# Attention scores of two pieces of keys, or of two groups of queries, in one visit of the matrix engine

## The chip, the core and the metric

The kernel runs on one core of a Trainium2 chip. The metric is device time in microseconds of the whole kernel, the median of the runs. Engines are called as in the profile: PE is the matrix engine (PEld its weight loads), DVE the vector engine, ACT the scalar engine, POOL the general-purpose engine, SP the engine whose queue issues the DMAs here. PSUM is the memory that PE writes to, in banks; SBUF is the working memory.

## What is computed

Four batches of 12480 tokens with 128 features, and 49 agents per batch, all in float32. Agents attend to the keys, queries attend to the agents, and the result runs through two matrices with a squared relu between them.

```
scale = 1 / sqrt(128)
def sm(a, b):
    s = scale * (a @ b.transpose(0, 2, 1))
    s = s - s.max(-1, keepdims=True)
    e = exp(s)
    return e / (e.sum(-1, keepdims=True) + 1e-9)
agent_v = sm(agents, k) @ v           # (4, 49, 128)
attn = sm(q, agents) @ agent_v        # (4, 12480, 128)
r = maximum(attn @ w_in, 0)           # w_in 128 x 2048
out = (r * r) @ w_out                 # w_out 2048 x 128
```

## The kernel before

**The tokens.** A batch is cut into `NS` = 13 pieces of 960 tokens (`G` = 8 columns of `CH` = 120 tokens). The same cut serves keys and values (pieces) and queries (groups; 52 of them over the four batches, `NSG`).

**The main loop** has one block per group of queries and per sixteenth of the hidden layer and half of the tokens: 52 x 16 = 832 blocks, called i. The product of `agent_v` and `w_in` is folded into one small matrix per batch (`w_make`), so that a block is: `mm1(i)` (L376, matmuls on L384), six matmuls from the softmax of the queries `PT` into a bank pair `h`; `relu(i)` on ACT (L390); after every second block `square` on ACT (L393), `high` on DVE (L397, a rounded copy) and `low` on DVE (L401, what the rounding left), each over the two blocks; and `mm2` (L403, matmuls on L412), twelve matmuls, five blocks behind `mm1` (`LAG`). After eight blocks one tile of the output is whole, and `store` (L414) takes it out with a copy on ACT (L417) and an addition on DVE (L418). `h` has two buffers, so `mm1(i)` needs `relu(i - 2)` to be through. `rg`, `gh` and `gl` have three.

**PSUM.** The output tiles use two bank pairs in turn, `pairs`; while one collects an output, the other is free for all other matmuls ("visits"), and `bank()` hands it out. So a visit's result has to be read before the next visit writes there.

**The work beside the main loop**, for which the visits are:
- *A piece of keys:* `k_load` (L158), `k_scores` (L168, through `scores`, L162, matmuls on L165: 8 columns in two halves of 64 and 56 tokens, 49 agents wide, into one bank), `k_copy` on ACT (L172) into the tile `sk`, `k_pmax` on DVE (L175), the maximum over the piece for every agent and partition. When the 13 pieces of a batch are there, `k_max` (L180) takes the maximum over them.
- *A piece of values:* `k_sub` on POOL (L197), `k_exp` and `k_hi` on ACT, `k_lo` on POOL (L207), `v_hi` on ACT, `v_lo` on DVE, `v_acc` on PE (L239), `v_sum` on DVE (L255).
- *A group of queries:* `q_load` (L298), `q_scores` (L302), then `q_shift` (L320), which is the maximum over the agents (`q_max`, L314) and its subtraction (`q_sub`, L318) on DVE; `q_exp` on ACT (L325); `q_inverse` on DVE (sum L329, two small steps L333 and L334); `q_norm` on POOL (L337, the multiplication); `q_hi` on ACT (L341, a rounded copy) and `q_lo` on POOL (L344, the rest); `q_transpose` on PE (L352) and `q_copy` on ACT (L356); `q_spread`, two DMAs.

**The order** is written out by a planner, and every engine runs its instructions in the order of emission. Each step gets a time in blocks (`at`), and the steps are emitted sorted by time. `chain` (L439) places a list of steps one behind the other, with `hop` (L431) as the least distance in blocks between two engines; each step of an engine takes one block's place on it (`taken`), and PE's visits stand only behind three blocks of every eight (`slots`). A step on PE and the readers of its bank (`reads_bank`, L474) are placed together: the last reader may stand at most one block later. A DVE step that reads a bank directly behind PE stands at +0.47 of PE's block, and the pair's `low` is then moved behind it (`read`, L625); other steps stand at +0.5, `high` at +0.6 and `low` usually at +0.65 of an odd block. `plan_tokens` (L476) places a group of queries, `plan_batch` (L486) a batch's keys and values. Before the loop stands a hand-timed prologue with the first batch's attention and groups 0 and 1 (L531 on).

Of the kernel before, what the change touches and what calls it, by code (L numbers as in the profile page):

```python
# [25 lines left out]
def agent_attention_relu2_kernel(ctx: ExitStack, tc: tile.TileContext, qT, kT, v, agT, w_in, w_out, outT):  # L26
# [29 lines left out]
    ag_sb = cpool.tile([P, B, A], F32, name="ag_sb")  # L56
# [81 lines left out]
    H = G // 2  # L138
# [16 lines left out]
    def piece(n):  # L155
        return sk[:, n * G:(n + 1) * G, :]
# [5 lines left out]
    def scores(ps, x, b, cs=range(G)):  # L162
        for c in cs:
            for r in rc:
                nc.tensor.matmul(ps[r, 0, c * A:(c + 1) * A], x[:, c, r], ag_sb[:, b, :], start=True, stop=True)  # L165
# [5 lines left out]
    def k_copy(n):
        nc.scalar.copy(piece(n), pss.pop(("k", n)))  # L172

    def k_pmax(n):
        nc.vector.tensor_reduce(out=pm[:, n, :], in_=piece(n).rearrange("p c a -> p a c"), axis=AX.X, op=ALU.max)  # L175

    def k_pmax_bank(n):
        nc.vector.tensor_reduce(out=pm[:, n, :], in_=pss["k", n].rearrange("p c a -> p a c"), axis=AX.X, op=ALU.max)  # L178

    def k_max(step):  # L180
        if step == 0:
            nc.vector.tensor_reduce(out=m1, in_=pm[:, :NS - 1].rearrange("p n a -> p a n"), axis=AX.X, op=ALU.max)
        elif step == 1:
            nc.vector.tensor_tensor(m1, m1, pm[:, NS - 1], op=ALU.max)
# [111 lines left out]
    PT, qs, es, mxs, sms, pps = {}, {}, {}, {}, {}, {}  # L296
# [5 lines left out]
    def q_scores(s):  # L302
        pss["q", s] = scores(bank(), qs.pop(s), s // NS)

    def q_scores_part(s, x):
        if x == 0:
            pss["q", s] = bank()
            scores(pss["q", s], qs[s], s // NS, range(H))
        else:
            pss["q", s] = scores(pss["q", s], qs.pop(s), s // NS, range(H, G))  # L310

    def q_max(s):
        mxs[s] = wk.tile([CH, G, 1], F32, name="mx")
        nc.vector.tensor_reduce(out=mxs[s], in_=pss["q", s], axis=AX.X, op=ALU.max)  # L314

    def q_sub(s):
        es[s] = wk.tile([CH, G, A], F32, name="e")
        nc.vector.tensor_tensor(es[s], pss.pop(("q", s)), mxs.pop(s).to_broadcast([CH, G, A]), op=ALU.subtract)  # L318
# [5 lines left out]
    def q_exp(s):
        nc.scalar.activation(es[s], es[s], AF.Exp, scale=scale)  # L325

    def q_sum(s):
        sms[s] = wk.tile([CH, G, 1], F32, name="sm")
        nc.vector.tensor_reduce(out=sms[s], in_=es[s], axis=AX.X, op=ALU.add)  # L329

    def q_inverse(s):
        q_sum(s)
        nc.vector.tensor_scalar_add(sms[s], sms[s], 1e-9)  # L333
        nc.vector.reciprocal(sms[s], sms[s])  # L334

    def q_norm(s, eng=nc.gpsimd):
        eng.tensor_tensor(out=es[s], in0=es[s], in1=sms.pop(s).to_broadcast([CH, G, A]), op=ALU.mult)  # L337

    def q_hi(s):
        pps[s] = ppb[s % 2]  # L340
        nc.scalar.copy(pps[s][:, :, :A], es[s])  # L341

    def q_lo(s, eng=nc.gpsimd):
        eng.tensor_tensor(out=pps[s][:, :, L:], in0=es.pop(s), in1=pps[s][:, :, :A].bitcast(F32), op=ALU.subtract)  # L344
# [25 lines left out]
    NSG = B * NS  # L370
# [287 lines left out]
```

## Time and profile before

| | |
|---|---|
| time, median of 3 runs | 1907.62 us (1907.6 to 1908.82) |
| the profiled execution: its own time | 1906.95 us |
| its span, first to last instruction | 1905.2 us |
| granted clock of PE | 0.999 |
| busy: PE, PEld | 1892.5 us (99%), 1669.1 us (88%) |
| busy: DVE, ACT, POOL | 1750.9 us (92%), 1721.8 us (90%), 355.3 us (19%) |
| DMA, mean over the span | 69 GB/s |

The profile is of one execution; its times lie on its own clock from the first instruction. Busy time counts an engine's instructions and not its waits. The groups have, per line, operation and shape, the count, the busy time, the mean of one in ns, and the idle time of the engine just before them with what ended it. A row of the timeline is start, duration, engine, line, operation, `out<-in` with sizes, and in brackets the idle time before it. The chain of waits is the work that ended last, followed back to what released it. A row of PE's waits has the waiting and the releasing group, the total in us, the number and the longest. The rows of one stretch of time have its length and the busy time and count of PE, PEld, DVE, ACT, POOL, then PE's clock, the share of DMA and GB/s.

### The profile page before, as it was taken

Reading aid. Unit: us, or ns where it says so; the run is one execution under the profiler, and the core shown is the slowest. Engines: PE = TensorE matmul, PEld = TensorE weight load, DVE = VectorE, ACT = ScalarE, POOL = GpSimd, SP = SyncE. Lnnn points to the kernel's source line nnn. Section 1 sums busy time; section 2 is a strip of 40 time slices with the busy share of each in tenths; the row PEclk is TensorE's granted clock in tenths of the full one; section 3 lists DMA queues with packets and bytes.
Section 4 is the critical chain, followed back from the end, with each engine's and each line's share of the span. In section 5 each row is a group of like instructions: output and inputs, shape, how many; then the busy total and the mean of one; then the engine's idle time right before and its main releaser. Section 6 shows DMA issues by size and latency. Waiting matters only on the chain.

```text
span 1905.2 us, 45852 instructions
## 1 busy us (share of the span) xinstructions
PE 1892.5 (99%) x20204; PEld 1669.1 (88%) x20204; DVE 1750.9 (92%) x1476; ACT 1721.8 (90%) x1809; POOL 355.3 (19%) x199
## 2 busy tenths in 40 slices
PE   9999999999999999999999999999999999999998
PEld 8788889988888998898888898998988888888888
DVE  7888999999889999999888999999989898989987
ACT  5788999998888999999888999999989999999997
POOL 0110233231012223324001223224201010000100
PEclk9999999999999999999999999999999999999999
DMA  9322222311331221211232121221211111111110
GB/s 369 107 71 82 83 63 62 92 42 51 104 98 41 81 63 53 75 57 57 79 97 62 57 75 52 66 79 41 64 36 35 50 33 53 36 36 53 35 38 22
DMA packets 44760, 130.95 MB, mean 69 GB/s; under 512 B 5034, under 2 KB 18474, under 8 KB 44562
## 3 DMA queue, kind: packets, MB, share of 16 engines
q1 hardware_dynamic: 44562, 128.04, 21.7%
q8 instruction: 158, 2.59, 0.6%
q14 instruction: 40, 0.33, 0.1%
HBM read 82.89 MB, written 25.56 MB: 57 GB/s over the span
## 4 chain that ended last, share of the span: by engine, by line
PE 96%; DVE 2%; DMA 1%; ACT 1%; issue 0%; SPq 0%; DVEq 0%
PE pair L412 57%; PE h L384 29%; PE pair L165 5%; PE pair L239 2%; PE pair L352 2%; DMA raw<-w_in 1%; DVE gl L401 0%; PE pair L290 0%; DMA kt<-kT 0%; DMA vt<-v 0%; DVE sk L197 0%; ACT rg L393 0%; DVE pm L178 0%; DVE cv L100 0%; DVE gh L397 0%; DVE cv L101 0%
## 5 line engine op out<-in xcount | busy, mean ns | idle before, releaser
L401 DVE TENSOR_TENSOR gl<-rg,gh 128x1920 fp32r<-128x1920 f32 x416 | 947.9, 2279 | 14.9 <-DVE gh L397 0.9
L390 ACT ACTIVATE rg<-h 128x960 f32<-128x960 f32 x832 | 804.5, 974 | 139.7 <-PE h L384 139.1
L393 ACT ACTIVATE rg<-rg 128x1920 f32<-128x1920 f32 x416 | 756.4, 1818 | 5.9
L412 PE MATMUL pair<-gh,wo_lo 64*128 64x480 f32 x3328 | 655.8, 378 | 0.0
L412 PE MATMUL pair<-gh,wo_hi 64*128 64x480 f32 x3328 | 654.7, 378 | 0.4 <-DVE gh L397 0.4
L397 DVE CAST gh<-rg 128x1920 fp32r<-128x1920 f32 x416 | 503.3, 1210 | 95.7 <-ACT rg L393 88.6
L384 PE MATMUL h<-p_a,w_hi 49*128 49x480 f32 x1664 | 511.8, 386 | 0.6 <-ACT rg L390 0.6
L412 PE MATMUL pair<-gl,wo_hi 64*128 64x480 f32 x3328 | 509.7, 376 | 1.8 <-DVE gl L401 1.8
L384 PE MATMUL h<-p_b,w_hi 49*128 49x480 f32 x1664 | 507.6, 385 | 0.0
L412 PEld LDWEIGHTS pair<-gh,wo_lo 64*128 64x128 f32 x3328 | 339.1, 186 | 36.3
L412 PEld LDWEIGHTS pair<-gh,wo_hi 64*128 64x128 f32 x3328 | 336.5, 184 | 37.6 <-DVE gh L397 0.8
L412 PEld LDWEIGHTS pair<-gl,wo_hi 64*128 64x128 f32 x3328 | 329.7, 184 | 44.0 <-DVE gl L401 4.2
L384 PEld LDWEIGHTS h<-p_a,w_hi 49*128 49x128 f32 x1664 | 291.1, 185 | 27.2 <-issue 2.4
L384 PE MATMUL h<-p_a,w_lo 49*128 49x480 f32 x832 | 311.1, 374 | 0.0
L384 PE MATMUL h<-p_b,w_lo 49*128 49x480 f32 x832 | 311.1, 374 | 0.0
L384 PEld LDWEIGHTS h<-p_b,w_hi 49*128 49x128 f32 x1664 | 293.1, 185 | 13.6
L337 POOL TENSOR_TENSOR e<-e,sm 120x392 f32<-120x392 f32 x51 | 80.7, 1582 | 1023.5 <-DVE sm L334 865.7
L384 PEld LDWEIGHTS h<-p_a,w_lo 49*128 49x128 f32 x832 | 152.6, 183 | 17.9
L384 PEld LDWEIGHTS h<-p_b,w_lo 49*128 49x128 f32 x832 | 152.7, 184 | 0.7
L344 POOL TENSOR_TENSOR pp<-e,pp 120x392 fp32r<-120x392 f32 x51 | 96.8, 1898 | 150.3 <-ACT pp L341 150.3
L207 POOL TENSOR_TENSOR pe<-sk,pe 120x392 fp32r<-120x392 f32 x39 | 76.5, 1962 | 253.3 <-ACT pe L204 253.3
L197 POOL TENSOR_TENSOR sk<-sk,mM 120x392 f32<-120x392 f32 x39 | 97.0, 2488 | 0.0
(112 smaller groups left out, 1170.9 us busy)
## 6 DMA issues: line engine op xcount, KB each, us to landing
vt<-v SPq DMA_DIRECT2D x52, 516.0 KB
kt<-kT SPq DMA_DIRECT2D x52, 480.0 KB
qt<-qT SPq DMA_DIRECT2D x52, 480.0 KB
outT<-ob SPq DMA_DIRECT2D x104, 240.0 KB
p_b<-p_a SPq DMA_DIRECT2D x104, 183.8 KB
raw<-w_in SPq DMA_DIRECT2D x4, 512.0 KB
raw<-w_out SPq DMA_DIRECT2D x4, 512.0 KB
ag_sb<-agT SPq DMA_DIRECT2D x1, 98.0 KB
```

The costliest lines, as they stand in the source:

```text
L165: nc.tensor.matmul(ps[r, 0, c * A:(c + 1) * A], x[:, c, r], ag_sb[:, b, :], start=True, stop=True)
L197: eng.tensor_tensor(out=piece(n), in0=piece(n), in1=m.rearrange("p (o a) -> p o a", o=1).to_broadcast([CH, G, A]), op=ALU.subtract)
L207: eng.tensor_tensor(out=pes[n][:, :, A:], in0=piece(n), in1=pes[n][:, :, :A].bitcast(F32), op=ALU.subtract)
L239: nc.tensor.matmul(pss["v", n][:A2, u, :VW], pe[rc[u], c, :], vs[rc[u], c], start=c == 0, stop=c == G - 1)
L337: eng.tensor_tensor(out=es[s], in0=es[s], in1=sms.pop(s).to_broadcast([CH, G, A]), op=ALU.mult)
L344: eng.tensor_tensor(out=pps[s][:, :, L:], in0=es.pop(s), in1=pps[s][:, :, :A].bitcast(F32), op=ALU.subtract)
L384: nc.tensor.matmul(h[:, u, :TT], w[ra[u], j, :], PT[s][u ^ lo][ra[u], cs, :], start=x == 0, stop=x == 2)
L390: nc.scalar.activation(rgs[p][:, x], hs.pop(i)[:, :, :TT], AF.Relu)
L393: nc.scalar.activation(rgs[p], rgs[p], AF.Square)
L397: nc.vector.tensor_copy(ghs[p], rgs[p])
L401: nc.vector.tensor_tensor(out=gls[p], in0=rgs.pop(p), in1=ghs[p].bitcast(F32), op=ALU.subtract)
L412: nc.tensor.matmul(outs[t][u][:, :TT], w[rg[u], 2 * j + e, :], g[rg[u], e, :], start=j == 0 and x == 0, stop=j == NJ - 1 and x == 5)
```

## The change

In the main loop, two pieces of keys, or two groups of queries, get their scores in one visit: the first in the first bank of the pair, the second in the second bank. Each reader then runs once over both: for keys the copy and the maximum, for queries the maximum, the subtraction, exp, the sum with its small steps, the multiplication, the rounded copy and the rest. The 13 pieces of a batch make six pairs and one single piece; groups 2 to 51 make 25 pairs. The transposes and the spreading remain one per group; for queries the two groups' softmax lies in two halves of the new tile `e` (in place of two rotating buffers) and of `pp`. `q_shift` is no longer one step of the loop's plan but two, `q_max` and `q_sub`, and both are readers of the bank. The loads of a pair are placed at one time. The maxima of the pieces in the loop are seven instead of thirteen. The prologue and group 1 work on one at a time, as before.

Its core:

```diff
-    ppb = [cpool.tile([CH, G, AW], F32R, name=f"pp{x}") for x in range(2)]
+    ppb = cpool.tile([CH, 2, G, AW], F32R, name="pp")
+    eb = cpool.tile([CH, 2, G, A], F32, name="e")
...
-    def k_scores(b, n):
-        pss["k", n] = scores(bank(), kts.pop((b, n)), b)
+    def both(ps, n):
+        return ps[:CH, :n, :G * A].rearrange("p u (c a) -> p u c a", a=A)
+
+    def k_scores(b, n, m=1):
+        ps = bank()
+        for u in range(m):
+            scores(ps, kts.pop((b, n + u)), b, u)
+        pss["k", n] = both(ps, m)
...
+    def q_scores(s, m=1):
+        ps = bank()
+        for u in range(m):
+            scores(ps, qs.pop(s + u), (s + u) // NS, u)
+        pss["q", s] = both(ps, m)
...
+    def hv(t, s, m):
+        return t[:, s % 2:s % 2 + m]
+
+    def q_exp(s, m=1):
+        nc.scalar.activation(hv(eb, s, m), hv(eb, s, m), AF.Exp, scale=scale)
...
-    reads_bank = (k_copy, k_max, v_sum, a_final, w_make, q_shift, q_copy)
+    reads_bank = (k_copy, k_max, v_sum, a_final, w_make, q_max, q_sub, q_copy)
 
     def plan_tokens(s, base):
-        todo = [("PE", q_scores, s), ("DVE", q_shift, s), ("ACT", q_exp, s), ("DVE", q_inverse, s),
-                ("POOL", q_norm, s), ("ACT", q_hi, s), ("POOL", q_lo, s),
-                ("PE", q_transpose, s), ("ACT", q_copy, s)]
-        first, end = chain(base, todo if s > 1 else todo[2:])
-        if s > 1:
-            at(first - 6, q_load, s)
-        at(end + .9, q_spread, s)
-        assert end + 3 < s * NF, (s, end)
+        m = min(s, 2)
+        todo = [("PE", q_scores, s, m), ("DVE", q_max, s, m), ("DVE", q_sub, s, m), ("ACT", q_exp, s, m), ("DVE", q_inverse, s, m),
+                ("POOL", q_norm, s, nc.gpsimd, m), ("ACT", q_hi, s, m), ("POOL", q_lo, s, nc.gpsimd, m)]
+        first, end = chain(base, todo if s > 1 else todo[3:])
+        end += 3
+        for x in range(s, s + m):
+            if s > 1:
+                at(first - 6, q_load, x)
+            _, e = chain(max(end, base + 9 + (x - s) * NF) if s > 1 else end, [("PE", q_transpose, x), ("ACT", q_copy, x)])
+            at(e + .9, q_spread, x)
+            assert e + 3 < x * NF, (x, e)
...
-        for n in range(NS):
-            first, t = chain(base + int(n * 4.6), [("PE", k_scores, b, n), ("ACT", k_copy, n), ("DVE", k_pmax, n)])
-            if b > 1 or n:
-                at(max(base - (6 if b > 1 else 0), first - 8), k_load, b, n)
-            if n == NS - 2:
-                chain(t + 1, [("DVE", k_max, 0)])
+        for n in range(0, NS, 2):
+            m = min(2, NS - n)
+            first, t = chain(base + int(n * 4.6), [("PE", k_scores, b, n, m), ("ACT", k_copy, n, m), ("DVE", k_pmax, n, m)])
+            for x in range(n, n + m):
+                if b > 1 or x:
+                    at(max(base - (6 if b > 1 else 0), first - 8), k_load, b, x)
+            if n + 3 == NS:
+                chain(t + 1, [("DVE", k_max, 0, NS // 2 + 1)])
...
-    for s in range(2, NSG):
+    for s in range(2, NSG, 2):
         plan_tokens(s, (s - 2) * NF + NF // 2 + LAG)
```

More of the change, by code (lines that the diff above doesn't have):

```diff
@@ L62, in agent_attention_relu2_kernel @@
     VW = 2 * C + 2
-    ppb = [cpool.tile([CH, G, AW], F32R, name=f"pp{x}") for x in range(2)]
-    for x in ppb:
-        nc.gpsimd.memset(x[:, :, A:L].bitcast(F32), 0.0)
+    ppb = cpool.tile([CH, 2, G, AW], F32R, name="pp")
+    for x in range(2):
+        nc.gpsimd.memset(ppb[:, x, :, A:L].bitcast(F32), 0.0)
+    eb = cpool.tile([CH, 2, G, A], F32, name="e")
     win_sb = cpool.tile([P, F], F32, name="win_sb")
@@ L160, in k_load, with scores, pieces, k_copy @@
         nc.sync.dma_start(out=kts[b, n], in_=kT[b, n])
-    def scores(ps, x, b, cs=range(G)):
+    def scores(ps, x, b, u=0, cs=range(G)):
         for c in cs:
             for r in rc:
-                nc.tensor.matmul(ps[r, 0, c * A:(c + 1) * A], x[:, c, r], ag_sb[:, b, :], start=True, stop=True)
-        return ps[:CH, 0, :G * A].rearrange("p (c a) -> p c a", a=A)
-    def k_scores(b, n):
-        pss["k", n] = scores(bank(), kts.pop((b, n)), b)
[L171 to L175, printed above, removed]
+                nc.tensor.matmul(ps[r, u, c * A:(c + 1) * A], x[:, c, r], ag_sb[:, b, :], start=True, stop=True)
+        return ps[:CH, u, :G * A].rearrange("p (c a) -> p c a", a=A)
+    def both(ps, n):
+        return ps[:CH, :n, :G * A].rearrange("p u (c a) -> p u c a", a=A)
+    def pieces(n, m):
+        return sk[:, n * G:(n + m) * G, :]
+    def k_scores(b, n, m=1):
[3 more added lines that the diff above has]
+        pss["k", n] = both(ps, m)
+    def k_copy(n, m=1):
+        nc.scalar.copy(pieces(n, m).rearrange("p (u c) a -> p u c a", u=m), pss.pop(("k", n)))
+    def k_pmax(n, m):
+        nc.vector.tensor_reduce(out=pm[:, n // 2, :], in_=pieces(n, m).rearrange("p c a -> p a c"), axis=AX.X, op=ALU.max)
     def k_pmax_bank(n):
-        nc.vector.tensor_reduce(out=pm[:, n, :], in_=pss["k", n].rearrange("p c a -> p a c"), axis=AX.X, op=ALU.max)
-    def k_max(step):
+        nc.vector.tensor_reduce(out=pm[:, n, :], in_=pss["k", n][:, 0].rearrange("p c a -> p a c"), axis=AX.X, op=ALU.max)
+    def k_max(step, np=NS):
         if step == 0:
-            nc.vector.tensor_reduce(out=m1, in_=pm[:, :NS - 1].rearrange("p n a -> p a n"), axis=AX.X, op=ALU.max)
+            nc.vector.tensor_reduce(out=m1, in_=pm[:, :np - 1].rearrange("p n a -> p a n"), axis=AX.X, op=ALU.max)
         elif step == 1:
-            nc.vector.tensor_tensor(m1, m1, pm[:, NS - 1], op=ALU.max)
+            nc.vector.tensor_tensor(m1, m1, pm[:, np - 1], op=ALU.max)
         elif step == 2:
@@ L294, in w_make @@
             nc.vector.tensor_tensor(wl[:, js], pss.pop(("w", b, j)), wh[:, js].bitcast(F32), op=ALU.subtract)
-    PT, qs, es, mxs, sms, pps = {}, {}, {}, {}, {}, {}
+    PT, qs, mxs, sms = {}, {}, {}, {}
     def q_load(s):
@@ L300, in q_load @@
         nc.sync.dma_start(out=qs[s], in_=qT[s])
-    def q_scores(s):
-        pss["q", s] = scores(bank(), qs.pop(s), s // NS)
+    def q_scores(s, m=1):
[3 more added lines that the diff above has]
+        pss["q", s] = both(ps, m)
     def q_scores_part(s, x):
@@ L307, in q_scores_part, with q_max, q_sub @@
             pss["q", s] = bank()
-            scores(pss["q", s], qs[s], s // NS, range(H))
+            scores(pss["q", s], qs[s], s // NS, 0, range(H))
         else:
[L310 to L318, printed above, removed]
+            scores(pss["q", s], qs.pop(s), s // NS, 0, range(H, G))
+            pss["q", s] = both(pss["q", s], 1)
+    def hv(t, s, m):
+        return t[:, s % 2:s % 2 + m]
+    def q_max(s, m=1):
+        mxs[s] = wk.tile([CH, 2, G, 1], F32, name="mx")
+        nc.vector.tensor_reduce(out=mxs[s][:, :m].rearrange("p u c o -> p u (c o)"), in_=pss["q", s], axis=AX.X, op=ALU.max)
+    def q_sub(s, m=1):
+        nc.vector.tensor_tensor(hv(eb, s, m), pss.pop(("q", s)), mxs.pop(s)[:, :m].to_broadcast([CH, m, G, A]), op=ALU.subtract)
     def q_shift(s):
@@ L322, in q_shift, with q_inverse, q_norm, q_hi @@
         q_sub(s)
[L324 to L344, printed above, removed]
+    def q_exp(s, m=1):
+        nc.scalar.activation(hv(eb, s, m), hv(eb, s, m), AF.Exp, scale=scale)
+    def q_inverse(s, m=1):
+        sms[s] = wk.tile([CH, 2, G, 1], F32, name="sm")
+        x = sms[s][:, :m]
+        nc.vector.tensor_reduce(out=x, in_=hv(eb, s, m), axis=AX.X, op=ALU.add)
+        nc.vector.tensor_scalar_add(x, x, 1e-9)
+        nc.vector.reciprocal(x, x)
+    def q_norm(s, eng=nc.gpsimd, m=1):
+        eng.tensor_tensor(out=hv(eb, s, m), in0=hv(eb, s, m), in1=sms.pop(s)[:, :m].to_broadcast([CH, m, G, A]), op=ALU.mult)
+    def q_hi(s, m=1):
+        nc.scalar.copy(hv(ppb, s, m)[:, :, :, :A], hv(eb, s, m))
+    def q_lo(s, eng=nc.gpsimd, m=1):
+        eng.tensor_tensor(out=hv(ppb, s, m)[:, :, :, L:], in0=hv(eb, s, m), in1=hv(ppb, s, m)[:, :, :, :A].bitcast(F32), op=ALU.subtract)
     def q_transpose(s):
         PT[s] = (wk.tile([P, G, CH], F32R, name="p_a"), wk.tile([P, G, CH], F32R, name="p_b"))
-        ps, pp = bank(), pps.pop(s)
+        ps, pp = bank(), ppb[:, s % 2]
         pss["t", s] = [ps[:AW, u, :G * n].rearrange("p (c n) -> p c n", n=n) for u, n in enumerate((L, CH - L))]
@@ L422, in agent_attention_relu2_kernel @@
     LAG = 5
-    AHEAD = 0
     steps = []
@@ L498, in plan_batch @@
+        _, t0 = chain(t + 1, [("DVE", k_max, 1, NS // 2 + 1), ("PE", k_max, 2), ("DVE", k_max, 3), ("PE", k_max, 4), ("DVE", k_max, 5)])
         free = {}
```

3 lines of the change are left out of this document (removed).

## The prediction

> **What bounds the kernel now.** I read the page first, then PE's own waits, then the chain of waits around single visits, then the timelines of DVE, ACT and POOL around one group of queries.
>
> ```profile
> PE 1892.5 (99%) x20204; PEld 1669.1 (88%) x20204; DVE 1750.9 (92%) x1476; ACT 1721.8 (90%) x1809; POOL 355.3 (19%) x199
> ...
> PE 96%; DVE 2%; DMA 1%; ACT 1%; issue 0%; SPq 0%; DVEq 0%
> ```
>
> ```profile
> PE pair L412 <- DVE gl L401: 1.8, 3, 1.1
> ...
> PE h L384 <- ACT rg L390: 0.6, 1, 0.6
> ```
>
> PE is the chain; it hardly waits for anyone. So the time falls by whatever PE stops spending, and rises by whatever PE is newly made to wait. DVE and ACT run at nine tenths: they have little room to be late.
>
> The chain of waits in order of time (start, us, what) around one visit for a piece of keys:
>
> ```profile
> 510.89 0.66 PE h L384 x6
> 511.55 1.31 PE pair L412 x12
> 512.86 1.06 PE pair L165 x30
> 513.92 0.85 PE h L384 x6
> 514.77 1.32 PE pair L412 x12
> 516.09 0.66 PE h L384 x6
> ```
>
> A block without a visit takes 0.66 + 1.31 = 1.97 us. From 510.89 to 516.09 two blocks and one visit take 5.20 us, so the visit costs 5.20 - 3.93 = 1.27: 1.06 of its own, 0.20 in the first matmuls behind it. How much of that is fixed? PE's timeline inside the visit, once cut off in its middle and once whole:
>
> ```profile
> 512.79 0.62 PE L165 MATMUL pair<-ag_sb,kt 128*64 128x49 f32 x15
> ...
> 512.79 1.13 PE L165 MATMUL pair<-ag_sb,kt 128*64 128x49 f32 x32
> ```
>
> The last 17 of the 32 instructions take 1.13 - 0.62 = 0.51 us, 0.030 each; 32 of them are 0.95. The rest, 1.27 - 0.95 = **0.32 us, is the price of going into the scores and back out**, paid per visit and not per piece.
>
> **What the merge takes off PE.** The loop has 39 visits for keys (3 batches of 13) and 50 for queries (groups 2 to 51): 89. Afterwards there are 3 x 7 and 25: 46. 43 visits fewer at 0.32 is **-13.8 us** (0.30 to 0.34 each: 12.9 to 14.6). Every matmul stays. The second piece needs its own load's semaphore; it was issued 6 to 8 blocks (12 us or more) earlier, so I cost that wait at nothing.
>
> **What it takes off the readers.** A doubled reader saves one start-up. The prices, grouped by line:
>
> ```profile
> L390 ACT ACTIVATE rg<-h 128x960 f32<-128x960 f32 x832 | 804.5, 974 | 139.7 <-PE h L384 139.1
> L255 DVE TENSOR_TENSOR acc<-pair,acc 98x516 f32<-98x516 f32 x36 | 24.8, 688 | 0.0
> L318 DVE TENSOR_TENSOR e<-pair,mx 120x392 f32<-120x392 f32 x51 | 28.9, 567 | 5.2
> L341 ACT CAST pp<-e 120x392 fp32r<-120x392 f32 x52 | 27.2, 523 | 0.0
> L175 DVE TENSOR_REDUCE pm<-sk 120x49 f32<-120x392 f32 x39 | 34.2, 877 | 1.1
> L182 DVE TENSOR_REDUCE m<-pm 120x49 f32<-120x588 f32 x4 | 4.9, 1217 | 0.0
> ```
>
> ACT: 960 columns against 392 give (974 - 523) / 568 = 0.8 ns a column, so 784 columns take 0.85 us where two took 1.05. DVE: 516 against 392 give 1.0 ns, so 0.97 us where two took 1.13. The maximum over a piece of keys (0.88 alone, 1.22 for 588 columns, both strided) becomes about 1.6 for two. All of it is beside PE; it is worth nothing by itself, and a longer single instruction is in the way for longer. So sum and place both matter.
>
> **What it moves: the chain of a query group.** Today `q_shift` is one step, right behind the scores, and exp and `q_inverse` follow one block later, emitted *ahead of* that block's `high` and `low` on DVE. Now max and subtraction are two steps, the subtraction one block later, so exp and `q_inverse` come in the second block after the scores, *behind* `high` and `low` of the pair between. POOL's multiply and ACT's `q_hi` still follow 1 and 3 blocks behind `q_inverse`. Here is one group today, 1491.87 being its scores: PE's chain, then DVE, POOL, ACT.
>
> ```profile
> 1491.87 1.06 PE pair L165 x30
> 1492.94 0.85 PE h L384 x6
> ...
> 1500.98 0.65 PE h L384 x6
> ...
> 1506.86 0.65 PE h L384 x6
> ```
>
> ```profile
> 1492.99 0.57 DVE L314 TENSOR_REDUCE mx<-pair 120x8 f32<-120x392 f32 x1 [0.21 <-PE pair L165]
> 1493.66 0.57 DVE L318 TENSOR_TENSOR e<-pair,mx 120x392 f32<-120x392 f32 x1
> 1494.14 2.15 DVE L401 TENSOR_TENSOR gl<-rg,gh 128x1920 fp32r<-128x1920 f32 x1
> 1496.21 0.56 DVE L329 TENSOR_REDUCE sm<-e 120x8 f32<-120x392 f32 x1
> 1496.80 0.17 DVE L333 TENSOR_SCALAR sm<-sm 120x8 f32<-120x8 f32 x1
> 1497.01 0.20 DVE L334 RECIPROCAL sm<-sm 120x8 f32<-120x8 f32 x1
> 1497.13 1.11 DVE L397 CAST gh<-rg 128x1920 fp32r<-128x1920 f32 x1
> 1498.27 2.68 DVE L401 TENSOR_TENSOR gl<-rg,gh 128x1920 fp32r<-128x1920 f32 x1
> ```
>
> ```profile
> 1497.36 1.58 POOL L337 TENSOR_TENSOR e<-e,sm 120x392 f32<-120x392 f32 x1 [27.86 <-DVE sm L334]
> 1501.92 1.04 POOL L344 TENSOR_TENSOR pp<-e,pp 120x392 fp32r<-120x392 f32 x1 [2.99 <-ACT pp L341]
> ```
>
> ```profile
> 1494.69 0.52 ACT L325 ACTIVATE e<-e 120x392 f32<-120x392 f32 x1
> ...
> 1501.33 0.52 ACT L341 CAST pp<-e 120x392 fp32r<-120x392 f32 x1
> 1501.74 0.97 ACT L390 ACTIVATE rg<-h 128x960 f32<-128x960 f32 x1
> 1502.75 1.81 ACT L393 ACTIVATE rg<-rg 128x1920 f32<-128x1920 f32 x1
> 1504.46 0.96 ACT L390 ACTIVATE rg<-h 128x960 f32<-128x960 f32 x1
> ```
>
> POOL is done at 1498.94; ACT comes to `q_hi` at 1501.33: 2.4 us to spare. Now the same group doubled, by these durations and the new order. PE's rows move by 0.95. DVE: max 1493.94 to 1494.92; `low` to 1497.1; subtraction to 1498.1; `high` (its square is done) to 1499.25; `low` (2.15) to 1501.4; sum 0.97 and the two small steps 0.44, to 1502.8. POOL starts 0.15 later (as at 1497.36), at 1502.95.
>
> The multiply over 784 columns is not in the trace. Its 1.58 today holds a wait: it starts while DVE's CAST runs and ends 0.70 after it (1498.24 to 1498.94). Another 392 columns add between that 0.70 and the whole 1.58; the nearest row is the 1.04 of POOL's other step beside the same work, so 2.6 (2.3 to 3.2). The Trainium skill (SBUF — State Buffer, "Who interferes with whom") has the two engines share a port pair that the first comer locks for its whole instruction. By that rule the wait is paid once and not doubled, which is 2.6 rather than 3.2, and DVE's next `low` stands still meanwhile; its 2.68 beside POOL, 2.15 alone, agrees.
>
> So POOL ends at 1505.55. The block that begins at 1500.98 + 0.95 = 1501.95 has its relu 0.8 later (1501.74 today), 0.97 long, so ACT is at `q_hi` by 1503.7: **it waits 1.9 us, for the first time, and the squares and relus queue behind it.** `q_hi` 0.85 to 1506.4, square (1.81, overlapping 0.1) to 1508.1, relu to 1509.05. That relu frees the bank for mm1, which PE reaches at 1506.86 + 0.95 = 1507.8. **PE waits 1.3 us** (2.3: 1.0; 3.2: 1.9). Were POOL's step no longer than today, it would wait 0.3.
>
> How many of the 25 pairs? Six have nothing but queries beside them, as here: 7.8 us. Thirteen stand among pieces of values, where POOL has more to do and DVE is fuller:
>
> ```profile
> 1060.00:1425.00 365.00, 365.00 (x3729) 326.52 (x3729) 348.10 (x290) 345.04 (x367) 97.66 (x46) 1.00 0.21 61
> ...
> L197 POOL TENSOR_TENSOR sk<-sk,mM 120x392 f32<-120x392 f32 x39 | 97.0, 2488 | 0.0
> ```
>
> DVE is busy 95% of these 365 us and POOL's subtraction holds it 2.5 us at a time; on the other side PE's visits for values give ACT and DVE time. I take 1.2 each: 15.6. Six stand among keys; where a double visit for keys (2 us) falls into the five blocks in between, PE arrives later than the relu and nothing is lost, elsewhere up to 1: I take 0.3 each, 1.8. Sum of the stalls +25.2 (25 pairs at 0.3 to 1.9: 7 to 48).
>
> **Other edits.** Loads come in pairs, up to 2 keys + 2 queries of the 5 buffers of `io`, and on SP two issues stand behind each other ahead of a store; with 6 blocks of lead I cost it at nothing, a late one at 1 to 2 us. The first maximum reads 6 columns per agent instead of 12, off PE's path. Prologue and group 1 do what they did: 0. The transposes stay where they were.
>
> **The sum.** The profiled execution took 1906.95 (span 1905.2); -13.8 + 25.2 gives 1918.4. The three runs' median is 0.67 above that execution: **1919 us**.
>
> **Rivals.**
> *The whole gain* (other side): POOL is through before ACT arrives, or a relu has room enough. It decides at a multiply of 0.7 us from DVE's reciprocal on for ACT not to wait, or 1.3 for PE not to. Against it is POOL's 1.58 for half the work; for it, any slip in the order I worked out (`q_inverse` ahead of `low` gives POOL 3 us more). 1906.95 - 13.8 + 0.67 = 1894.
> *Worse than forecast*: `low` behind the multiply grows from 2.68 by another 1.04, and POOL's `q_lo`, doubled, then shuts out the next CAST, so second matmuls wait for `gl` too; among values POOL is behind its 2.5 us step. Some 0.9 more in 19 pairs: 1936.
> *The bank is held*: the subtraction reads both banks until 1498.1, and a visit two blocks after the scores could begin at 1493.9 + 2.17 + 1.97 = 1498.0. 0.1 to 0.9 us (`low` ahead of it slowed by POOL) at perhaps 10 places, on top of the forecast: 1924. The Trainium skill (Perfetto Trace Analysis, "Matmuls") wants independent matmul groups to rotate through banks so that one's readers overlap the next one's matmuls; this change gives up that second bank. No row of today shows such a wait.
> *It does not do what it says*: the second piece waits inside its visit, or the way in is paid again at the second bank; the gain is gone as are most of the stalls: 1907.
>
> **Chances.** Forecast 0.45, whole gain 0.26, worse 0.14, bank 0.06, no merge 0.09. 0.2% is 3.8 us, about what a measurement can tell. Of the forecast, with POOL's bounds and the thirteen pairs among values in doubt, 0.36 lies slower, 0.06 within, 0.03 faster. Slower 0.36 + 0.14 + 0.06 = 0.56; same 0.06 + 0.09 = 0.15; faster 0.03 + 0.26 = 0.29. The range runs from the whole gain to the worse case, 1895 to 1936; the forecast's own is 1908 to 1930.
>
> **What would show it.** Right: L165 in half as many visits of 2.0 us with 0.85 behind each; the multiply on POOL near 2.6; a new row of ACT's copy into `pp` waiting for POOL, 20-odd times near 1.9; PE's `h` waiting for ACT's `rg`, in total near 25. Wrong: no such row, and PE still waiting for nobody: then the time is 1894. If the visits are 2.3 or more, or PE waits for `kt` or `qt`, the merge itself failed.

## The result, and the profile after

The changed kernel takes **1928.57 us** in the median of five runs (1926.65 to 1931.37), beside 1908.44 (1907.60 to 1909.39) for the kernel before on the same chip: a ratio of 1.0105, interval 1.0091 to 1.0120. It is 20.1 us slower. The forecast was 1919, in a range of 1895 to 1936. The profiled execution took 1928.57 itself (span 1926.8, granted clock 0.996), 21.6 more than that of before.

Line numbers have moved: the scores are on L166 (L165 before), `mm1` L397 (L384), relu L403 (L390), square L406 (L393), `high` L410 (L397), `low` L414 (L401), `mm2` L425 (L412), the store's copy and addition L430 and L431 (L417, L418), the query's steps L331 to L357 (L314 to L344), the transposes L365 (L352).

The page after: busy time and the chain by engine.

```profile
PE 1895.7 (98%) x20204; PEld 1666.8 (87%) x20204; DVE 1740.5 (90%) x1333; ACT 1720.0 (89%) x1741; POOL 288.1 (15%) x149
PE 81%; DVE 9%; ACT 6%; issue 3%; POOL 1%; DMA 0%; POOLq 0%; ACTq 0%; DVEq 0%
```

DVE, ACT and POOL are busy for less time in all, and yet 16% of the chain now run through them (3% before). That is not a matter of load but of single instructions that end too late. The waits of the changed kernel (total us, times, longest):

```profile
PEld h L397 <- ACT rg L403: 16.4, 21, 1.1
ACT pp L354 <- POOL e L351: 15.5, 17, 1.5
PEld pair L425 <- DVE gl L414: 10.3, 11, 2.0
PEld pair L365 <- issue: 9.6, 7, 1.7
PE pair L365 <- DVE ob L431: 7.0, 6, 1.4
PE h L397 <- ACT rg L403: 6.3, 13, 0.7
PE pair L425 <- DVE gl L414: 5.7, 7, 1.6
```

A stall shows twice, once for the weight load (PEld) and once, shorter, for the matmul behind it. I add up the PEld rows alone. There are three kinds: matmuls that wait for a relu (16.4), second matmuls that wait for `gl` (10.3) and transposes (9.6, whose matmuls name the store's addition on DVE). Together they are 36.3; before, the same three rows gave 2.2 + 4.2 + 0.8 = 7.2, here with a fourth row:

```profile
PEld pair L412 <- DVE gl L401: 4.2, 7, 1.5
PEld h L384 <- ACT pp L341: 2.4, 3, 0.8
PEld h L384 <- ACT rg L390: 2.2, 3, 1.0
PEld pair L352 <- issue: 0.8, 4, 0.2
```

The fourth row matters because of a change of names. In both kernels the six visits that make the next batches' matrices (`w_make`) are each followed by a wait of 0.8. Before, three of them are put down to `pp`; in the changed kernel two of them are put down to the relu. So 1.6 of the 16.4 is not new, and the relu row grew by 12.6.

**The visit itself does what was forecast.** The chain around a double visit for keys (start, us, what):

```profile
506.65 1.32 PE pair L425 x12
507.98 2.00 PE pair L166 x61
509.97 0.85 PE h L397 x6
```

It takes 2.00 where a single one took 1.06, and the 0.85 behind it is paid once for two: by these rows 2 x 1.06 + 0.20 - 2.00 = 0.32 us saved. Measured over all visits of the two traces, from the `mm2` ahead to the `mm2` behind, a single visit lengthens a block by 1.27 in the median and a double one by 2.20, which is 0.34 saved. I take 0.333 us per visit, 14.3 for 43 visits (forecast 13.8). The whole loss is in stalls, and in the clock that falls after some of them.

**Beside queries alone** the forecast's chain of events can be read row by row. This is one pair in the changed kernel, 1544.15 being its scores: DVE, POOL, ACT and PE.

```profile
1549.16 0.97 DVE L334 TENSOR_TENSOR e<-pair,mx 120x784 f32<-120x784 f32 x1
...
1553.31 0.96 DVE L346 TENSOR_REDUCE sm<-e 120x16 f32<-120x784 f32 x1
...
1555.88 3.27 DVE L414 TENSOR_TENSOR gl<-rg,gh 128x1920 fp32r<-128x1920 f32 x1
1559.76 2.15 DVE L410 CAST gh<-rg 128x1920 fp32r<-128x1920 f32 x1 [0.61 <-ACT rg L406]
```

```profile
1554.91 2.23 POOL L351 TENSOR_TENSOR e<-e,sm 120x784 f32<-120x784 f32 x1 [61.52 <-PE h L397]
1558.10 2.79 POOL L357 TENSOR_TENSOR pp<-e,pp 120x784 fp32r<-120x784 f32 x1 [0.97 <-ACT pp L354]
```

```profile
1557.17 0.86 ACT L354 CAST pp<-e 120x784 fp32r<-120x784 f32 x1 [1.27 <-POOL e L351]
1557.93 1.80 ACT L406 ACTIVATE rg<-rg 128x1920 f32<-128x1920 f32 x1
1559.64 0.94 ACT L403 ACTIVATE rg<-h 128x960 f32<-128x960 f32 x1
```

```profile
1557.57 0.60 PE L425 MATMUL pair<-gl,wo_hi 64*128 64x480 f32 x4
1558.01 0.38 PE L397 MATMUL h<-p_a,w_hi 49*128 49x480 f32 x1
...
1559.54 0.60 PE L425 MATMUL pair<-gl,wo_hi 64*128 64x480 f32 x4
1560.63 0.49 PE L397 MATMUL h<-p_a,w_hi 49*128 49x480 f32 x1 [0.49 <-ACT rg L403]
```

POOL ends at 1557.14, ACT has waited 1.27 for it, relu is through at 1560.58, and PE's next matmul starts at 1560.63. One block earlier the step from the four matmuls to the next is 0.44, here it is 1.09: PE loses 0.65 us at this step, where 1.3 were forecast. Each POOL step also holds DVE up: `low` lasts 3.27 and the CAST 2.15, beside 2.15 and 1.15 alone. In sum DVE loses nothing by it: all `low` and CAST together take 1450 us, 1451 before. What has grown is the longest single one, `low` from 3.05 to 3.84 and CAST from 1.93 to 2.46.

**Among values** it is another story, which the forecast had only as its rival "worse". DVE and POOL of the changed kernel:

```profile
248.58 2.46 DVE L410 CAST gh<-rg 128x1920 fp32r<-128x1920 f32 x1
251.07 2.80 DVE L414 TENSOR_TENSOR gl<-rg,gh 128x1920 fp32r<-128x1920 f32 x1
253.80 2.39 DVE L241 TENSOR_TENSOR vs<-vt,vs 120x512 fp32r<-120x512 f32 x1
256.11 1.15 DVE L410 CAST gh<-rg 128x1920 fp32r<-128x1920 f32 x1
257.17 0.64 DVE L431 TENSOR_TENSOR ob<-ob,pair 128x480 f32<-128x480 f32 x1
```

```profile
248.26 1.75 POOL L351 TENSOR_TENSOR e<-e,sm 120x784 f32<-120x784 f32 x1 [10.82 <-DVE sm L348]
249.98 1.88 POOL L207 TENSOR_TENSOR sk<-sk,mM 120x392 f32<-120x392 f32 x1
251.82 3.81 POOL L357 TENSOR_TENSOR pp<-e,pp 120x784 fp32r<-120x784 f32 x1
```

Three POOL steps stand one behind the other for 7.4 us. DVE's CAST, `low` and the values' `v_lo` (at 253.80; 0.84 in the mean of its 78) take 7.6 instead of 4.1. So the store's addition comes only at 257.17, and the transposes behind it, which need its bank, start at 257.96 instead of about 256.4 (256.00 and the 0.44 that such a step takes). Then the clock falls; its rows stand at the end.

### The profile page after: what moved, and what is told of

Same layout as the page of the kernel before. It is cut to its first block, busy times and chain, and to the rows that moved or that the text cites. A ratio compares the mean times of both kernels' runs of the same rounds, so it can differ in the third digit from the quotient of the medians.

```text
span 1926.8 us, 45526 instructions
## 1 busy us (share of the span) xinstructions
PE 1895.7 (98%) x20204; PEld 1666.8 (87%) x20204; DVE 1740.5 (90%) x1333; ACT 1720.0 (89%) x1741; POOL 288.1 (15%) x149
## 4 chain that ended last, share of the span: by engine, by line
PE 81%; DVE 9%; ACT 6%; issue 3%; POOL 1%; DMA 0%; POOLq 0%; ACTq 0%; DVEq 0%
PE pair L425 47%; PE h L397 24%; PE pair L166 5%; ACT rg L406 3%; DVE gl L414 2%; ACT rg L403 2%; DVE gh L410 2%; PE pair L365 2%; PE pair L249 2%; POOL e L351 1%; DVE vs L241 1%; DVE sm L346 1%; PE pair L539 1%; DVE e L334 0%; DVE mx L331 0%
## 5 line engine op out<-in xcount | busy, mean ns | idle before, releaser
L414 DVE TENSOR_TENSOR gl<-rg,gh 128x1920 fp32r<-128x1920 f32 x416 | 932.0, 2240 | 17.6 <-DVE gh L410 1.4
L403 ACT ACTIVATE rg<-h 128x960 f32<-128x960 f32 x832 | 798.2, 973 | 146.6 <-PE h L397 145.8
L406 ACT ACTIVATE rg<-rg 128x1920 f32<-128x1920 f32 x416 | 756.5, 1819 | 7.1
L425 PE MATMUL pair<-gh,wo_hi 64*128 64x480 f32 x3328 | 656.8, 378 | 0.4 <-DVE gh L410 0.4
L425 PE MATMUL pair<-gh,wo_lo 64*128 64x480 f32 x3328 | 655.2, 377 | 0.0
L410 DVE CAST gh<-rg 128x1920 fp32r<-128x1920 f32 x416 | 518.0, 1245 | 100.4 <-ACT rg L406 92.1
L425 PE MATMUL pair<-gl,wo_hi 64*128 64x480 f32 x3328 | 516.2, 380 | 5.9 <-DVE gl L414 5.7
L397 PE MATMUL h<-p_a,w_hi 49*128 49x480 f32 x1664 | 508.4, 385 | 6.6 <-ACT rg L403 6.3
L397 PE MATMUL h<-p_b,w_hi 49*128 49x480 f32 x1664 | 507.8, 385 | 0.0
L425 PEld LDWEIGHTS pair<-gh,wo_lo 64*128 64x128 f32 x3328 | 341.5, 186 | 39.1
L425 PEld LDWEIGHTS pair<-gl,wo_hi 64*128 64x128 f32 x3328 | 329.4, 184 | 49.4 <-DVE gl L414 10.3
L425 PEld LDWEIGHTS pair<-gh,wo_hi 64*128 64x128 f32 x3328 | 338.8, 185 | 38.2 <-DVE gh L410 0.8
L397 PEld LDWEIGHTS h<-p_a,w_hi 49*128 49x128 f32 x1664 | 293.9, 186 | 40.5 <-ACT rg L403 16.4
L397 PE MATMUL h<-p_b,w_lo 49*128 49x480 f32 x832 | 313.6, 377 | 0.0
L397 PE MATMUL h<-p_a,w_lo 49*128 49x480 f32 x832 | 313.4, 377 | 0.0
L397 PEld LDWEIGHTS h<-p_b,w_hi 49*128 49x128 f32 x1664 | 296.3, 186 | 15.9
L351 POOL TENSOR_TENSOR e<-e,sm 120x784 f32<-120x784 f32 (+1 forms) x26 | 50.8, 1952 | 895.2 <-PE h L397 371.5
L397 PEld LDWEIGHTS h<-p_a,w_lo 49*128 49x128 f32 x832 | 153.6, 185 | 15.3
L397 PEld LDWEIGHTS h<-p_b,w_lo 49*128 49x128 f32 x832 | 153.6, 185 | 3.1
L207 POOL TENSOR_TENSOR sk<-sk,mM 120x392 f32<-120x392 f32 x39 | 80.3, 2058 | 87.3 <-DVE mM L204 87.3
L357 POOL TENSOR_TENSOR pp<-e,pp 120x784 fp32r<-120x784 f32 (+1 forms) x26 | 75.3, 2898 | 29.9 <-ACT pp L354 29.9
```

The costliest lines, as they stand in the source:

```text
L207: eng.tensor_tensor(out=piece(n), in0=piece(n), in1=m.rearrange("p (o a) -> p o a", o=1).to_broadcast([CH, G, A]), op=ALU.subtract)
L351: eng.tensor_tensor(out=hv(eb, s, m), in0=hv(eb, s, m), in1=sms.pop(s)[:, :m].to_broadcast([CH, m, G, A]), op=ALU.mult)
L357: eng.tensor_tensor(out=hv(ppb, s, m)[:, :, :, L:], in0=hv(eb, s, m), in1=hv(ppb, s, m)[:, :, :, :A].bitcast(F32), op=ALU.subtract)
L397: nc.tensor.matmul(h[:, u, :TT], w[ra[u], j, :], PT[s][u ^ lo][ra[u], cs, :], start=x == 0, stop=x == 2)
L403: nc.scalar.activation(rgs[p][:, x], hs.pop(i)[:, :, :TT], AF.Relu)
L406: nc.scalar.activation(rgs[p], rgs[p], AF.Square)
```

## The experiments

Each edit is to the changed kernel, unless it says otherwise. To compare them I keep one account for all profiled executions: the three PEld waits, the stretches of half clock (3.41 us each, so 1.7 us lost; the last one of a run, after the work, not counted), and 0.333 us per visit saved. "Account" is the sum minus 7.2, plus 1.7 for each stretch beyond the one of before, minus the visits saved; beside it stands the profiled execution's time minus 1906.95.

| kernel | relu + `gl` + transposes, us | half clock | visits saved | account | measured |
|---|---|---|---|---|---|
| before | 2.2 + 4.2 + 0.8 | 1 | 0 | | |
| changed | 16.4 + 10.3 + 9.6 | 4 | 43 | +19.9 | +21.6 |
| keys only | 2.2 + 5.0 + 0.4 | 0 | 18 | -7.3 | -2.8 |
| queries only | 19.4 + 8.5 + 4.4 | 1 | 25 | +16.8 | +19.5 |
| later | 5.9 + 20.6 + 2.5 | 2 | 43 | +9.2 | +13.2 |
| one step | 4.7 + 38.1 + 2.6 | 8 | 43 | +35.8 | +43.2 |
| later transposes | 15.2 + 21.9 + 1.8 | 0 | 43 | +15.7 | +17.0 |
| halves | 50.6 + 5.4 + 3.3 | 16 | 43 | +63.3 | +61.5 |
| single tails | 6.9 + 11.6 + 5.9 | 0 | 43 | +1.2 | -0.2 |
| tails, one step | 3.3 + 12.5 + 1.2 | 1 | 43 | -4.5 | +1.1 |
| tails, later transposes | 6.4 + 13.1 + 0.9 | 0 | 43 | -2.8 | -2.0 |
| mixed | 5.2 + 10.3 + 1.0 | 0 | 38 | -5.1 | -2.4 |
| before, more POOL | 14.4 + 12.3 + 2.1 | 1 | 0 | +21.6 | +14.0 |

Seven of twelve agree within 3 us. "Later", "one step" and "tails, one step" have besides one wait of 3.9, 4.6 and 3.4 us for the spread softmax of a group. Keys alone and the kernel with more POOL work are 4 to 8 us off. Some of the agreement is luck: the relu column holds up to four of the six waits behind `w_make` (two of 0.8 in the changed kernel, four in "queries only" and "single tails"). Without them only five of twelve agree, and ten of twelve lie below the measured time, the changed kernel at +18.3. So the account is good to some 6 us, is 8 to 10 off in two rows, and part of what the merge costs stands in none of its columns.

**Which half of the change: keys only.** Queries one at a time with their one-step shift, as before (queries only is its counterpart: keys one at a time).

```diff
-        m = min(s, 2)
+        m = 1
...
-    for s in range(2, NSG, 2):
+    for s in range(2, NSG):
```

> Only the keys are merged (18 double visits fewer singles in the loop), the queries stay one group at a time in the order of before. The theory (the loss comes from the merged query chain, where ACT's q_hi waits for POOL and POOL's doubled steps shut DVE out): the 18 merged visits give their 0.33 us each and nothing is lost, 1908.4 - 6 = 1902 to 1903. The rival (any doubled reader, put into one place, makes the pair's low or a relu late): keys lose too, 1908 to 1914. A second rival (most of the loss is in the keys): 1915 and more.

1904.41 us (1903.28 to 1905.42), ratio 0.9983 (0.9973 to 0.9992): faster by 3.2, of the 6 for 18 visits. That is 1.4 short of what the theory had. No new wait is among its rows, so where the other 3 stay is open.

> Only the queries are merged, the keys stay one piece at a time in the order of before. The theory: all of the loss and 25 x 0.33 = 8 us of the gain, 1928.6 + 6 = 1934 to 1936. The rival (doubled readers hurt wherever they are): the loss is shared, 1917 to 1922.

1925.86, ratio 1.0099 (1.0084 to 1.0114), between the theory's and the rival's times. Merging queries alone brings nearly all of the loss, though 25 of 43 visits are theirs. Yet the halves do not add up: -3.2 and +18.2 make 15.0, the whole change costs 20.1. The difference is about the size of the three stretches of half clock (5.1) that the changed kernel has more than this one.

**Is it the wait of ACT for POOL? Later.** `q_hi` and `q_lo` two blocks later, the transposes behind them.

```diff
-        first, end = chain(base, todo if s > 1 else todo[3:])
+        if s > 1:
+            first, end = chain(base, todo[:-2])
+            _, end = chain(end + 2 + 2, todo[-2:])
+        else:
+            first, end = chain(base, todo[3:])
```

> The whole change, but q_hi and q_lo stand two blocks later behind POOL's multiplication (5 blocks behind q_inverse instead of 3), the transposes two blocks later too. If ACT waiting for POOL is the loss, ACT's copy into pp waits no more, the regular stall of 0.66 us per pair among queries alone is gone, and the time is 1896 to 1902. If POOL's doubled steps shutting DVE out of the port are the larger part, the stalls among values stay: 1912 to 1922. If neither, 1928.

1920.45, ratio 1.0068 (1.0053 to 1.0083). ACT's wait for POOL is gone from the rows, and the wait for relu falls from 16.4 to 5.9. But PE's wait for `gl` doubles:

```profile
PEld pair L425 <- DVE gl L414: 20.6, 21, 2.5
```

The sum of the three falls by 7.3 only, and 3.4 more come from two stretches of half clock less; one new wait of 3.9 for the spread softmax works against them. The forecast's mechanism is real and its removal is worth less than half of the loss.

**Is it the place behind `low`? One step.** Maximum and subtraction in one step, so exp and `q_inverse` stand one block earlier, ahead of `high` and `low`.

```diff
-        todo = [("PE", q_scores, s, m), ("DVE", q_max, s, m), ("DVE", q_sub, s, m), ("ACT", q_exp, s, m), ("DVE", q_inverse, s, m),
+        todo = [("PE", q_scores, s, m), ("DVE", q_shift, s, m), ("ACT", q_exp, s, m), ("DVE", q_inverse, s, m),
...
```

> The whole change, but maximum and subtraction of the queries stand as one step right behind the scores, as before the change, so that exp, q_inverse and POOL come one block earlier and ahead of high and low. If the place of q_inverse behind low is the loss, POOL is through 2 us before ACT arrives: 1895 to 1902. If the length of POOL's doubled steps is, wherever they stand, 1912 to 1925. If the two longer DVE steps ahead of low make gl late, PE waits for gl and the time is above 1915 with such rows.

1945.97, ratio 1.0198 (1.0181 to 1.0215): the slowest but one. I had put the blame on that place, and this falls. The third expectation fits the number, but its cause, two longer DVE steps ahead of `low`, falls with the one-step tails below. ACT no longer waits for POOL, but now both POOL steps meet a `low`. DVE of this kernel:

```profile
1570.50 3.34 DVE L414 TENSOR_TENSOR gl<-rg,gh 128x1920 fp32r<-128x1920 f32 x1
1573.77 1.15 DVE L410 CAST gh<-rg 128x1920 fp32r<-128x1920 f32 x1
1575.02 3.68 DVE L414 TENSOR_TENSOR gl<-rg,gh 128x1920 fp32r<-128x1920 f32 x1
```

Two in a row last 1.2 and 1.5 us longer than the 2.15 of one alone, and PE waits 38.1 us for `gl`.

**Does POOL's work cost time when nobody waits for its result? Before, more POOL.** The kernel before, with one more POOL instruction of 294 columns, whose result nothing uses, behind each `q_norm` and each `q_lo` of groups 2 to 51: 100 instructions of extra work.

```diff
         eng.tensor_tensor(out=es[s], in0=es[s], in1=sms.pop(s).to_broadcast([CH, G, A]), op=ALU.mult)
+        if s > 1:
+            eng.tensor_tensor(out=spare, in0=es[s][:, :6], in1=es[s][:, :6], op=ALU.mult)
... (the same behind q_lo)
```

> The kernel before the change, with one POOL instruction more behind each multiplication and one more behind each q_lo (294 columns, two inputs, into a spare tile that nobody reads): extra work that is not in the reference, 100 instructions of some 0.8 us on an engine that is idle four fifths of the time. No other engine waits for them except through a shared port. If POOL's work shuts DVE out, DVE's CAST and low beside them get longer by up to 0.8 each and PE waits for gl: 1914 to 1935. If there is no such effect, 1908.

1920.19, ratio 1.0067 (1.0052 to 1.0082): 12.8 us lost to results that nothing reads. But the experiment does not isolate DVE. The extra instructions also make POOL's own later steps late, and ACT waits for one of these, the subtraction among values, as it never did before:

```profile
ACT sk L200 <- POOL sk L197: 14.6, 10, 1.9
PEld h L390 <- ACT rg L396: 14.4, 19, 1.0
PEld pair L418 <- DVE gl L407: 12.3, 13, 1.5
```

Of the 19 waits for a relu, 16 (12.1 us) come within 8 us behind eight of those waits of ACT: two behind each. Six of the waits for `gl` (7.6 us; before, this row had 4.2 in all) are DVE's: ahead of each a CAST of 2.0 and a `low` of 2.5 stand beside the extra POOL instruction. So idle POOL work costs time in both ways, and the larger part here goes by ACT. In the mean `low` is no longer than before (2279 ns in both), CAST is (1264 beside 1210).

**Is it the length of one POOL instruction? Halves.** POOL's two doubled steps each cut in two, one directly behind the other.

```diff
-        eng.tensor_tensor(out=hv(eb, s, m), in0=hv(eb, s, m), in1=sms.pop(s)[:, :m].to_broadcast([CH, m, G, A]), op=ALU.mult)
+        sm = sms.pop(s)
+        for u in range(m):
+            x = hv(eb, s + u, 1)
+            eng.tensor_tensor(out=x, in0=x, in1=sm[:, u:u + 1].to_broadcast([CH, 1, G, A]), op=ALU.mult)
... (q_lo is cut in the same way)
```

> The changed kernel with POOL's doubled multiplication and doubled rest each cut into two instructions of one group, directly one behind the other at the same place; all else as changed. Theory A (what costs is that one doubled instruction shuts DVE out for twice as long): DVE gets in between the halves, no instruction of DVE lasts longer than in the kernel before (2.7 us for the rest gl), and the time falls by 5 to 12 us from the changed kernel's 1928.6, to 1916 to 1923. Theory B (what costs is that twice the POOL work falls in one place, in whatever pieces): ACT waits as long for POOL's second half, DVE is shut out twice in a row, and the time stays at 1926 to 1931.

1968.48, ratio 1.0320 (1.0306 to 1.0334): slower by another 40, which neither theory had. DVE, POOL, ACT, and the waits of this kernel:

```profile
1573.21 1.10 DVE L414 CAST gh<-rg 128x1920 fp32r<-128x1920 f32 x1
1574.41 2.60 DVE L418 TENSOR_TENSOR gl<-rg,gh 128x1920 fp32r<-128x1920 f32 x1
```

```profile
1573.43 4.28 POOL L354 TENSOR_TENSOR e<-e,sm 120x392 f32<-120x392 f32 x2 [62.29 <-DVE sm L348]
```

```profile
1577.75 0.86 ACT L357 CAST pp<-e 120x784 fp32r<-120x784 f32 x1 [3.33 <-POOL e L354]
```

```profile
ACT pp L357 <- POOL e L354: 50.7, 21, 3.5
PEld h L401 <- ACT rg L407: 50.6, 29, 3.2
```

DVE does get in between: `low` is down from 3.27 to 2.60, and the longest of all is 2.91. But then POOL's second half waits out that `low` as well: it ends at 1577.71, 0.70 behind the `low`, and lasts 2.76 where the first half lasts 1.56. The two take 4.28 where one doubled instruction took 2.23. ACT waits 3.33 instead of 1.27, and PE pays nearly all of it. So theory A was right on DVE, and the price of its cure is larger than its gain. About half of the 40 is the clock: at a mean of 0.986, (1 - 0.986) x 1966 = 27.5 us are lost; in the changed kernel, at 0.996, it is 7.7.

**The transposes: later transposes.** Only these, two blocks later.

```diff
-        end += 3
+        end += 3 if s == 1 else 5
```

> The whole change with the transposes alone placed two blocks later (the next slot), nothing else moved. In the changed kernel PE waits there for the store's addition on DVE, 7 us in all, 6 times. If those waits are a cause of their own, they go and with them some clock: 1918 to 1922. If they only show that DVE is late anyway, the same lateness appears as waits for gl: 1925 to 1930.

1923.49, ratio 1.0084 (1.0069 to 1.0099), between the two expectations. The transposes' wait goes (9.6 to 1.8), and the wait for `gl` takes its place (10.3 to 21.9): PE stands still as long as in the changed kernel (38.9 beside 36.3 in the three rows), only in smaller pieces. The 5 us gained are those of the clock, which no longer falls at all. So the store's bank is where late DVE work shows first, not a cause of its own.

**Merge in front, not behind: single tails.** Scores, maximum, subtraction, exp and sum stay merged. Multiplication, copy and rest come once per group, the second group's 16 blocks later.

```diff
-        first, end = chain(base, todo if s > 1 else todo[3:])
...
+        if s > 1:
+            first, end = chain(base, todo[:-3])
+            for x in (s, s + 1):
+                _, ends_at[x] = chain(end + 1 + (x - s) * NF, [("POOL", q_norm, x), ("ACT", q_hi, x), ("POOL", q_lo, x)])
...
```

> The whole change up to q_inverse (one visit, one maximum, subtraction, exp and sum for two groups, keys merged too), but the tail of the chain, POOL's multiplication, q_hi and q_lo, runs once per group as before, the second group's 16 blocks after the first's. If POOL's doubled steps (ACT waiting for them, DVE shut out of the port by them) are the loss, all visits saved are a gain now: 1894 to 1902. If the doubled DVE and ACT readers in front, or the place of q_inverse, are the loss, it stays at 1915 or more.

1907.21, ratio 0.9999 (0.9990 to 1.0009): the whole loss is gone, but none of the gain is there, of which at least 5 us had been expected. Stalls of 0.2 to 0.9 us remain at some 30 places, and they use up what the 43 visits save. This edit changes two things, the length of POOL's steps and how far apart they stand; "halves" changed the length alone and was slower, so the length alone is not it. With the one-step shift as well:

> As the run with single tails, but maximum and subtraction as one step right behind the scores. If what made that one-step order slow was POOL's doubled steps standing where DVE's low follows at once, it is now like the single tails, 1894 to 1904. If it was the two long DVE steps ahead of low, PE still waits for gl and it is 1912 or more.

1908.51, ratio 1.0006 (0.9997 to 1.0016), above the one expectation and below the other. The order that cost 17 us with doubled POOL steps costs 1.3 with single ones.

**And the transposes later on top of that; and what is left among values.**

> Keys and scores of queries merged, with multiplication, rounded copy and rest on their own for each of the two groups (as in the kernel of single tails), and now the transposes two blocks later. There, PE's short stalls sum up to some 9 us more than before: six of 0.7 us at transposes that wait for the store's addition on DVE, and some 15 of 0.3 to 0.4 at gl. Theory (the place of the transposes makes the first kind and delays what follows): the six go, and perhaps half of the second kind behind them: 4 to 6 us less than the single tails, 1901 to 1904 beside 1907.6 before. Rival (DVE is simply fuller in one place, because the doubled maximum, subtraction and sum come together, and gl is late whatever the transposes do): 1906 to 1908.

1905.58, ratio 0.9987 (0.9978 to 0.9995): faster than before by 2.5, between the two expectations. The transposes' waits are gone (5.9 to 0.9), those at `gl` are not (11.6 to 13.1). Five stalls of 1.2 us remain at `gl`, between 622 and 907 us: one for each of the pairs among the second set of values in the loop.

> As the kernel with single tails and later transposes, and ACT's rounded copy and POOL's rest stand two blocks later behind POOL's multiplication. With single tails ACT still waits for POOL nine times, 5.4 us in all, and PE for a relu ten times, 6.9. Theory (ACT's wait is what is left of the stalls): those two rows go, and the time falls by a further 2 to 4 us, to 1898 to 1902. Rival (the stalls that are left come from DVE alone): equal to the kernel with single tails and later transposes within 1 us.

1905.33. This tells nothing of its theory: `q_hi` stood two blocks behind POOL already, so the order of all instructions is the same, and it only shows how well a time repeats. For the last one, groups 16 to 25 go one at a time:

```diff
+        for x in (s, s + 1) if 16 <= s < 26 else (s,):
+            plan_tokens(x, (x - 2) * NF + NF // 2 + LAG, 1 if 16 <= s < 26 else 2)
```

> Keys merged; scores of queries merged with single tails and later transposes, but the ten groups 16 to 25, whose work lies beside the values of the second batch, one at a time as before. Where all groups were merged, five stalls of 1.2 us at gl remained, one for every one of these pairs, and little else. Theory (the doubled front is harmless where DVE has room and costs 1.2 where POOL's steps for values and a doubled group come together): -6.1 for the stalls, +1.65 for five visits more at 0.33 us: 1901 to 1902.5 beside 1908 before, the fastest of all versions. Rival (the values' steps make these stalls wherever the group is placed, or they move elsewhere): 1904.5 to 1908.

1904.42, ratio 0.9981 (0.9973 to 0.9990). The five stalls are gone, but two others of 1.2 us have come among the third set of values, beside one of 0.8 that stood there already, as the rival had it: the time is 1.9 above the theory's 1902.5 and 0.1 below the rival's range. This and merging keys alone, 3.2 to 3.7 us below before, are the fastest versions found. So merging the queries' scores brought nothing that these runs can tell from merging keys alone.

## Why the forecast was right in its sign and short in its size

- *PE is the chain and has no slack; 0.32 us per visit saved.* Right: 0.32 to 0.34 and some 14 us. Keys alone kept 3.2 of their 6.
- *POOL's multiplication.* Forecast 2.6 (2.3 to 3.2), measured 2.23 beside queries alone: below the range. The step of the forecast that took 1.04 for the second half is mis-sized; it was 0.65. The Trainium skill (SBUF — State Buffer, "Who interferes with whom") has the first comer keep the shared port pair for its whole instruction. The runs agree with the forecast's conclusion that the wait is then paid once: 2.23 for one doubled instruction, 4.28 for two halves with a `low` between them.
- *ACT waits for POOL, the relu is late, PE waits.* The mechanism is right, as the rows at 1554 to 1560 show, and "later" and "halves" move it down and up. The size was not: 17 waits of at most 1.5 instead of 20-odd near 1.9, 0.65 us for PE instead of 1.3, and 12.6 in all instead of 25.2. Of the 0.63 by which ACT's wait beside queries alone was too long, 0.37 is POOL's step; the rest is mostly DVE, which had its sums ready 10.61 behind the scores, not 10.93. Among values, where 15.6 was taken without a row that shows it, this kind of wait came to 4.8.
- *Doubled readers beside PE are worth nothing by themselves.* Right for the front: with single tails, maximum, subtraction, exp and sum remain doubled, and the loss is gone; but so is the gain.
- *What failed is the place of the rival "worse".* It had been given 0.14, as something that happens instead of the forecast. It happened besides it: POOL's doubled steps shut out `low`, CAST and `v_lo` for 1.0 to 1.6 us each. They make most of the wait at `gl`: 8.2 of its 10.3 us lie among values, where before it had 1.2.
- *"The transposes stay where they were", at no cost.* Wrong. Their place did stay; what was late was the store's addition that frees their bank: 9.6 us. The forecast followed DVE's lateness to `gl` and not to the other reader in its queue.
- *The clock* was not in the sum: three stretches more, 5.1 us.
- *The bank held by the subtraction*: 1.2 us in two places, as good as nothing. *No merge*: refuted by the visits of 2.00.

So the sum on the changed kernel's own rows is 36.3 - 7.2 + 5.1 - 14.3 = +19.9, beside 21.6 in the profile (+18.3 without the two renamed waits). The forecast's +25.2 for stalls was 33 to 34 with the clock, of which under half came by the way it described. That the time came out near the forecast is in part luck: its one term for stalls was twice too large, and three terms that it did not have (`gl`, the transposes, the clock) filled the place.

## What to carry to other kernels

When two small jobs are merged to save the bounding engine a fixed price, merge at most the steps that write or read its bank, and look at every later step on an engine that shares something with a full one. Here merging the front paid for itself and no more, and doubling POOL's two steps and the copy between them cost some 20 us on top, though POOL is busy 15% of the time and runs fewer instructions over the same columns. Ask of each instruction that grows not only who waits for its result, but who stands still while it runs, and then follow *all* that stands behind that one in its queue. Cutting the long instruction is no cure where somebody waits for its last piece.

## What the hardware showed that I had not expected

**The clock falls after short stalls, not only after idle time.** Windows of the changed kernel (stretch, length, busy time and count of PE, PEld, DVE, ACT, POOL, then PE's clock, DMA share, GB/s):

```profile
256.04:259.45 3.41, 2.06 (x28) 1.66 (x26) 3.41 (x4) 2.13 (x3) 1.20 (x1) 1.00 0.20 72
259.45:262.86 3.41, 3.41 (x21) 3.12 (x20) 3.38 (x3) 3.06 (x4) 3.08 (x2) 0.50 0.02 5
399.39:402.80 3.41, 2.42 (x24) 1.80 (x22) 3.41 (x2) 3.38 (x4) 3.11 (x2) 1.00 0.00 0
907.99:911.40 3.41, 1.80 (x18) 1.24 (x16) 3.41 (x3) 3.41 (x5) 1.02 (x2) 1.00 0.00 0
911.40:914.81 3.41, 3.41 (x28) 2.98 (x26) 3.41 (x3) 1.52 (x2) 0.56 (x1) 0.50 0.19 72
1136.68:1140.09 3.41, 2.04 (x28) 1.67 (x26) 3.41 (x3) 1.97 (x3) 1.36 (x1) 1.00 0.19 72
```

All the stretches of half clock lie on one grid of 3.41 us (259.45, 911.40 and 1140.09 are 191 and 67 steps apart). Laid on that grid, the three windows of the loop in which PE was busy least, 1.80, 2.04 and 2.06 us of 3.41, are the three that were followed by half clock; the next, 2.42, was not. The same count over the profiles of the thirteen kernels of the table, some 7300 windows: each of the 23 in which PE was busy for at most half was followed by half clock, of 16 between 50% and 61% six were, and of those that were busier none was, as long as it ran at full clock itself. Five windows at half clock (four of them in "halves") were followed by a second one although PE was never idle in them. So a stall of about 1.5 us, if it fell into one window, could cost 1.7 us on top of itself here. The Trainium skill (TensorE: Matmul & The Clock Gate, "What's actually happening") gives a free-running window of 3413 ns and half rate, and the runs agree; it has the clock fall after at least one idle window, and here PE was busy for more than half of each of the three. What the gate counts is not shown by these runs.
